# One block of zeros one place sooner, and the first load in two halves: a recurrence with a mixture of experts behind it

## The chip, the cores and the metric

The kernel runs on one core of a Trainium2 chip. The metric is the device time of one execution in microseconds (us); 213.54 us is the median of three runs before the change (213.47 to 214.17).

## The reference

What is computed is a gated recurrence over four sequences of 5056 tokens with 256 features, followed by a mixture of eight experts on its 20224 rows. Each expert keeps the 80 rows with the largest gate; all other rows of the output are zero.

```python
sig = 1.0 / (1.0 + np.exp(-f_logit))
f = lower_bound + (1.0 - lower_bound) * sig
for t in range(S):                      # h, y: (4, 256) at each t
    h = f[:, t] * h + (1.0 - f[:, t]) * x[:, t]
    y[:, t] = h
x = y.reshape(20224, 256)
logits = x @ w_gate                     # 8 experts
expert_idx = argmax(logits); gate_w = softmax(logits)[expert_idx]
out = zeros
for e in range(8):
    tok = the 80 tokens of expert e with the largest gate_w
    out[tok] = gate_w[tok] * (relu(x[tok] @ w1[e]) @ w2[e])
```

## The kernel before, in words

The first stage runs over 40 units of 512 tokens of one sequence. For each, "load" (line 233) issues two DMAs of 512 KB on SyncE's queue, f_logit into a tile f_t and x into a tile x_t, each of 128 partitions with 4 KB; eight ring slots hold them, so four units are loaded ahead. ScalarE takes the sigmoid (L242), GpSimd multiplies (L246), TensorE turns both (L252, L260), ScalarE forms the decay (L269) and VectorE scans (L277). Two small loads (w_gate and lower_bound, L215 and L217) stand behind the loads of unit 1; TensorE's first work, small_t (L223), turns them.

The output is some 20.7 MB and nearly all zero. One block of 512 KB is written from on-chip zeros by "clear"; "copied" (L132) copies it over the rest of the output, DRAM to DRAM, a block per call, and the calls are spread over the whole kernel as DMAs on SyncE's queue. The very last block is 256 KB.

The second stage ranks the rows (lines 496 to 703). The third, "experts" (L717), runs over the eight experts. The weights come as 32 halves of 512 KB, numbered k = 0 to 31 in the order in which they are loaded: w1 of expert 0, then, for each e, w1 of expert e+1 and w2 of expert e. Half k goes into ring slot 1 + k mod 7, so it waits for the reader of half k-7. Hence k = 26 and 27 are w1 of expert 7, 28 and 29 are w2 of expert 6, and 30 and 31 are w2 of expert 7 (31 is issued as two DMAs of 256 KB). "more" (L791) issues the next two halves, and behind half k as many blocks of zeros as BETWEEN (L530) names k; this list is the order written out by hand. "hidden" multiplies by w1 (L755), "relu" follows on ScalarE (L762) and VectorE (L763), "result" multiplies by w2 (L770), "finish" scales on VectorE (L778). At the end GpSimd issues eight "scatter"s (L783), indirect DMAs that write the 80 rows of each expert into the output; the code demands that all zeros are written by then. Scatters of experts 5 and 6 stand besides behind a matmul of result(7).

Work of one engine runs in the order in which the program issues it, and so do DMAs of SyncE's queue.

Of the kernel before, what the change touches and what calls it, by code (L numbers as in the profile page):

```python
# [17 lines left out]
P = 128  # L18
# [8 lines left out]
def kernel(  # L27
# [11 lines left out]
    nc = tc.nc  # L39
# [17 lines left out]
    def first(g):  # L57
        return g * G
# [27 lines left out]
    def slot(i, name):  # L86
        return ring[i].tile([P, R * D], F32, name=name, tag="buf")
# [44 lines left out]
    def copied():  # L132

        at = written[0]
        n = min(P * ZH, TOTAL - at)
        if n:
            z = 2 * ZH if n % (2 * ZH) == 0 else D
            nc.sync.dma_start(out=out_flat[ds(at, n)].rearrange("(p k) -> p k", k=z),
                              in_=out_flat[:n].rearrange("(p k) -> p k", k=z))
            written[0] += n  # L140
# [14 lines left out]
    def tiles(ap, b, g):  # L155
        return ap[b, ds(min(first(g), S - G), G)].rearrange("(p r) d -> p r d", r=R)
# [6 lines left out]
    with tc.tile_pool(name="gsm", bufs=1) as gsm:  # L163
# [3 lines left out]
        xs, fs, sts, uts, sps, ups, lgs, lss, lts, eqs = ({} for _ in range(10))  # L167
# [65 lines left out]
        def load(n):  # L233
            g, b = divmod(n, B)
            fs[n] = slot(2 * n % NSLOT, "f_t").rearrange("p (r d) -> p r d", r=R)
            nc.sync.dma_start(out=fs[n], in_=tiles(f_logit, b, g))
            xs[n] = slot((2 * n + 1) % NSLOT, "x_t").rearrange("p (r d) -> p r d", r=R)
            nc.sync.dma_start(out=xs[n], in_=tiles(x, b, g))

# [163 lines left out]
        with tc.tile_pool(name="plg", bufs=1, space=PSUM) as plg, \  # L403
             tc.tile_pool(name="plt", bufs=1, space=PSUM) as plt:
            with tc.tile_pool(name="pss", bufs=2, space=PSUM) as pss, \
                 tc.tile_pool(name="psu", bufs=3, space=PSUM) as psu:
                for n in range(-AHEAD, n_unit):
                    unit(load, n + AHEAD)
                    m = n + AHEAD
                    if m == 1:  # L410
# [34 lines left out]
                    if n > 0 and n % B == 0:  # L445
                        g = n // B - 1
# [7 lines left out]
            with tc.tile_pool(name="pct", bufs=4, space=PSUM) as pct:  # L454
                cts = {}

                def turn(*runs):
                    ct = pct.tile([P, 4 * P], F32, name="ct", tag="ct")
                    for g0, g1 in runs:
                        turned(ct[:, ds((g0 - runs[0][0]) * P, (g1 - g0) * P)], g0, g1)  # L460
                        cts[g0] = ct, runs[0][0]
                    return ct
# [18 lines left out]
                b = turn((4, 6))  # L481
# [44 lines left out]

    w_sb = {}
    RANKING = 12
    BETWEEN = (7, 8, 8, 14, 15, 20, 21, 25, 28)
    for k, key in enumerate(halves_of[:NSLOT - 1]):  # L530
        w_sb[key] = half(*key)
        copied()
# [184 lines left out]
    def experts(again):  # L717
        with tc.tile_pool(name="mp", bufs=2) as mp, \
# [72 lines left out]
            def more(m):  # L791
                for _ in range(2 * m):
                    if late:
# [3 lines left out]
                        if not again:  # L797
                            for _ in range(BETWEEN.count(k)):
                                copied()
# [44 lines left out]
    with tc.If(unsure > 0):  # L844
        with tc.tile_pool(name="all", bufs=1) as sel, \
# [31 lines left out]
            for e in range(E):  # L877
                nc.gpsimd.indirect_dma_start(
                    out=tok[:, ds(e, 1)], out_offset=None, in_=id_list,
# [54 lines left out]
```

## Time and profile before

| What | us |
|---|---|
| median of three runs | 213.54 |
| the profiled execution, its own time | 212.61 |
| its span, first to last instruction | 210.8 |
| TensorE busy | 178.6 (85%) |
| VectorE busy | 156.0 (74%) |
| GpSimd busy | 143.2 (68%) |
| ScalarE busy | 133.4 (63%) |

The profile is of one execution. PE is TensorE's matmuls, PEld its weight loads, DVE is VectorE, ACT is ScalarE, POOL is GpSimd and SP is SyncE; a "q" behind a name is that engine's queue, which hands work out. A tile name with an arrow, as w_sb<-in_moe_w_dram, is what an instruction writes and reads. In brackets behind an instruction stands the idle time of its engine and what ended it. All times count from the start of the span. The queue of hardware DMAs moved 79.45 MB, which is 94.1% of what 16 DMA engines' time allows over the span.

### The profile page before, as it was taken

Reading aid. Unit: us, or ns where it says so; the run is one execution under the profiler, and the core shown is the slowest. Engines: PE = TensorE matmul, PEld = TensorE weight load, DVE = VectorE, ACT = ScalarE, POOL = GpSimd, SP = SyncE. Lnnn points to the kernel's source line nnn. Section 1 sums busy time; section 2 is a strip of 40 time slices with the busy share of each in tenths; the row PEclk is TensorE's granted clock in tenths of the full one; section 3 lists DMA queues with packets and bytes.
Section 4 is the critical chain, followed back from the end, with each engine's and each line's share of the span. In section 5 each row is a group of like instructions: output and inputs, shape, how many; then the busy total and the mean of one; then the engine's idle time right before and its main releaser. Section 6 shows DMA issues by size and latency. Waiting matters only on the chain.

```text
span 210.8 us, 6578 instructions
## 1 busy us (share of the span) xinstructions
PE 178.6 (85%) x2091; PEld 140.2 (66%) x2091; DVE 156.0 (74%) x399; ACT 133.4 (63%) x420; POOL 143.2 (68%) x287
## 2 busy tenths in 40 slices
PE   0499989997999999989999886689999697989870
PEld 0498868785878778777878763355586475767540
DVE  5159969999998999899798999975678756461010
ACT  4279789797787778777979872615666555360000
POOL 4848779799797889769897982416666565620372
PEclk9999999999999999999999999797999999999998
DMA  5999999999999999999999999999999999999621
GB/s 214 419 364 398 411 419 448 386 444 394 410 409 414 384 423 375 399 450 386 433 375 408 428 393 371 419 414 432 424 403 404 424 404 420 413 408 410 237 74 51
DMA packets 21362, 80.60 MB, mean 382 GB/s; under 512 B 2580, under 2 KB 2710, under 8 KB 20888
## 3 DMA queue, kind: packets, MB, share of 16 engines
q1 hardware_dynamic: 20936, 79.45, 94.1%
q0 software_dynamic: 384, 0.66, 1.1%
q8 instruction: 18, 0.29, 0.5%
q14 instruction: 24, 0.20, 0.2%
HBM read 72.62 MB, written 21.36 MB: 446 GB/s over the span
## 4 chain that ended last, share of the span: by engine, by line
DMA 34%; PE 33%; ACT 11%; DVE 8%; issue 5%; POOL 4%; ACTq 1%; POOLq 0%; SPq 0%; DVEq 0%
DMA w_sb<-in_moe_w_dram 19%; PE sp L252 11%; PE up L260 9%; DMA x_t<-in_x_dram 8%; PE lg L290 6%; DMA f_t<-in_f_logit_dram 6%; ACT h_all L269 5%; PE lt L314 2%; ACT xe L735 2%; POOL x_t L246 2%; DVE h_all L277 2%; ACT ls L299 2%; PE y_ps L770 2%; POOL out_dram L783 2%; PE h_ps L755 1%
## 5 line engine op out<-in xcount | busy, mean ns | idle before, releaser
L246 POOL TENSOR_TENSOR x_t<-f_t,x_t 128x1024 f32<-128x1024 f32 x40 | 94.8, 2373 | 21.1 <-DMA x_t<-in_x_dram 12.5
L277 DVE TENSOR_TENSOR_SCAN h_all<-h_all,up 128x512 f32<-128x512 f32 (+1 forms) x80 | 95.8, 1245 | 10.4 <-PE up L260 6.5
L269 ACT ACTIVATE h_all<-sp,nomlb 128x512 f32<-128x512 f32 (+1 forms) x80 | 50.3, 678 | 13.6 <-PE sp L252 12.8
L242 ACT ACTIVATE f_t<-f_t 128x1024 f32<-128x1024 f32 x40 | 42.4, 1059 | 11.6 <-DMA f_t<-in_f_logit_dram 9.8
L260 PE MATMUL up<-ident,x_t 128*128 128x128 f32 x320 | 43.8, 279 | 3.1 <-DVE h_all L277 1.8
L252 PE MATMUL sp<-ident,f_t 128*128 128x128 f32 x320 | 45.4, 287 | 0.0
L252 PEld LDWEIGHTS sp<-ident,f_t 128*128 128x128 f32 x320 | 35.9, 145 | 7.7 <-issue 7.3
L260 PEld LDWEIGHTS up<-ident,x_t 128*128 128x128 f32 x320 | 37.0, 144 | 5.0 <-DVE h_all L277 2.9
L735 ACT COPY xe<-h_all 128x2 f32 x256 | 25.4, 191 | 14.6 <-issue 14.1
L735 POOL COPY xe<-h_all 128x2 f32 x192 | 24.4, 187 | 14.6 <-issue 8.3
L770 PE MATMUL y_ps<-w_sb,hid 128*80 128x256 f32 x128 | 29.5, 382 | 4.6 <-DMA w_sb<-in_moe_w_dram 4.6
L735 DVE COPY xe<-h_all 128x2 f32 x192 | 22.6, 176 | 12.2 <-issue 11.0
L770 PEld LDWEIGHTS y_ps<-w_sb,hid 128*80 128x80 f32 x128 | 18.4, 150 | 13.5 <-issue 3.4
L290 PE MATMUL lg<-h_all,wg 128*32 128x128 f32 (+1 forms) x640 | 26.5, 282 | 0.8 <-ACT ls L299 0.6
L755 PEld LDWEIGHTS h_ps<-xe,w_sb 128*64 128x64 f32 x512 | 18.3, 138 | 5.7 <-issue 3.0
L755 PE MATMUL h_ps<-xe,w_sb 128*64 128x80 f32 x512 | 19.5, 234 | 1.0 <-DMA w_sb<-in_moe_w_dram 0.6
L290 PEld LDWEIGHTS lg<-h_all,wg 128*32 128x32 f32 x640 | 15.4, 108 | 7.2 <-issue 4.9
L783 POOL DMA_INDIRECT out_dram<-y,goal x8 | 7.5, 939 | 11.1 <-DMA w_sb<-in_moe_w_dram 9.0
L161 PE MATMUL warm<-h_all,ident 128*128 128x512 f32 x18 | 11.9, 807 | 0.0
L778 DVE TENSOR_SCALAR y<-y_ps,gates 80x256 f32<-80x256 f32 x8 | 3.8, 477 | 10.9 <-PE y_ps L770 10.5
L762 ACT ACTIVATE hid<-h_ps 128x320 f32<-128x320 f32 x8 | 3.5, 435 | 11.3 <-PE h_ps L755 5.8
L314 PE MATMUL lt<-ident,ls 128*128 128x128 f32 (+1 forms) x40 | 7.3, 306 | 3.7 <-ACT ls L299 3.7
(128 smaller groups left out, 98.8 us busy)
## 6 DMA issues: line engine op xcount, KB each, us to landing
f_t<-in_f_logit_dram SPq DMA_DIRECT2D x40, 512.0 KB, 6.4
x_t<-in_x_dram SPq DMA_DIRECT2D x40, 512.0 KB, 6.9
w_sb<-in_moe_w_dram SPq DMA_DIRECT2D x31, 512.0 KB, 9.9
out_dram<-out_dram SPq DMA_DIRECT2D x26, 512.0 KB, 9.8
out_dram<-zbuf SPq DMA_DIRECT2D x12, 512.0 KB, 10.4
out_dram<-h_all SPq DMA_DIRECT2D x1, 512.0 KB, 8.2
w_sb<-in_moe_w_dram SPq DMA_DIRECT2D x2, 256.0 KB, 8.8
out_dram<-out_dram SPq DMA_DIRECT2D x1, 256.0 KB, 9.4
```

What stands on the lines that cost most here:

```text
L161: nc.tensor.matmul(warm, ident, h_all[:, 0, :4 * P], start=True, stop=True)
L242: nc.scalar.activation(s_t, s_t, ACT.Sigmoid, scale=-1.0)
L246: nc.gpsimd.tensor_tensor(u_t, sts[n], u_t, ALU.mult)
L252: nc.tensor.transpose(ps[:, ds(r * P, P)], sts[n][:, r, ds(o * P, P)], ident)
L260: nc.tensor.transpose(ps[:, r::R], uts[n][:, r, ds(o * P, P)], ident)
L269: nc.scalar.activation(columns(n, o).rearrange("p (k r) -> p k r", r=R), sps.pop((n, o)).rearrange("p (r k) -> p k r", r=R)[:, P - run(n / ...
L277: nc.vector.tensor_tensor_scan(h, h, ups.pop((n, o)), h_all[:, o, ds(spot(n - B) + G - 1, 1)] if n >= B else 0.0, ALU.mult, ALU.add)
L290: nc.tensor.matmul(lgs[g][ds(q * LC, LC), b, :k].rearrange("p (m i) -> p m i", i=2), wg[:, o], pairs[:, :, q], start=o == 0, stop=o == DC ...
L735: copy(X[e][:, :, ds(k + j, 1)], h_all[:, :, ds(v, 1)])
L755: nc.tensor.matmul(ps[i][ds(s * H, H), c], wo[o][:, at:at + J * (H - 1) + 1:J], xt[:, o], start=o == 0 and c == 0, stop=o == DC - 1, skip_ ...
L770: marks[e, c] = nc.tensor.matmul(y, hid[:, c], halves[c // CH][:, c % CH], start=c == 0, stop=c == FC - 1, skip_group_check=True)
L783: sent.append(nc.gpsimd.indirect_dma_start(out=out, out_offset=bass.IndirectOffsetOnAxis(ap=goal[:, ds(e, 1)], axis=0), in_=rows.pop(e), i ...
```

## The change

Two places differ. In BETWEEN the last number goes from 28 to 27, so the last block of zeros is issued behind half 27 and ahead of half 28. In "load", f_logit of unit 0 is loaded with two DMAs, of partitions 0 to 63 and of 64 to 127; all other loads are as they were.

```diff
-            nc.sync.dma_start(out=fs[n], in_=tiles(f_logit, b, g))
+
+            for p in range(0, P, P // 2 if n == 0 else P):
+                part = ds(p, P // 2 if n == 0 else P)
+                nc.sync.dma_start(out=fs[n][part], in_=tiles(f_logit, b, g)[part])
...
-    BETWEEN = (7, 8, 8, 14, 15, 20, 21, 25, 28)
+    BETWEEN = (7, 8, 8, 14, 15, 20, 21, 25, 27)
```

## Rows read from the trace of the kernel before

**Rows 1.** The page: span, DMA share in 40 slices, the scatters' DMA queue.

```profile
span 210.8 us, 6578 instructions
...
DMA  5999999999999999999999999999999999999621
...
q0 software_dynamic: 384, 0.66, 1.1%
```

**Rows 2.** The chain of waits from 186 us: start, us, what.

```profile
177.06 10.18 DMA w_sb<-in_moe_w_dram
...
188.74 9.88 DMA w_sb<-in_moe_w_dram
```

**Rows 3.** Timeline of GpSimd from 188.5: start, us, instruction, idle before it.

```profile
197.72 1.13 POOL L783 DMA_INDIRECT out_dram<-y,goal  x1 [8.96 <-DMA w_sb<-in_moe_w_dram]
199.15 0.92 POOL L783 DMA_INDIRECT out_dram<-y,goal  x1 [0.30 <-issue]
...
206.45 0.91 POOL L783 DMA_INDIRECT out_dram<-y,goal  x1 [0.30 <-issue]
```

**Rows 4.** Tile out_dram, DMAs issued from 187 to 188: issue to landing.

```profile
DMA to landing us min/median/max: 9.4/9.4/9.4
```

**Rows 5.** Line 783, instructions from 196 to 197.6: GpSimd's queue.

```profile
L783 POOLq EVENT_SEMAPHORE  x2: 42/42/43, 196.7 to 196.8; - x2
```

**Rows 6.** Timeline of SyncE's queue from 183 to 212.

```profile
183.46 1.95 SPq L517 DMA_DIRECT2D w_sb<-in_moe_w_dram  x2
186.80 0.38 SPq L523 DMA_DIRECT2D w_sb<-in_moe_w_dram  x1
187.26 0.52 SPq L138 DMA_DIRECT2D out_dram<-out_dram  x1
188.74 3.86 SPq L523 DMA_DIRECT2D w_sb<-in_moe_w_dram  x4
```

**Rows 7.** Tile w_sb, the DMA issued at 183.46 (k=26): issue to landing.

```profile
DMA to landing us min/median/max: 10.0/10.0/10.0
```

**Rows 8.** Timeline of all engines from 193: ScalarE, TensorE, VectorE.

```profile
195.58 0.44 ACT L762 ACTIVATE hid<-h_ps 128x320 f32<-128x320 f32 x1 [5.77 <-PE h_ps L755]
...
196.06 1.93 PE L770 MATMUL y_ps<-w_sb,hid 128*80 128x256 f32 x8
...
198.75 5.38 PE L770 MATMUL y_ps<-w_sb,hid 128*80 128x256 f32 x24 [0.76 <-DMA w_sb<-in_moe_w_dram]
...
204.17 0.48 DVE L778 TENSOR_SCALAR y<-y_ps,gates 80x256 f32<-80x256 f32 x1 [2.97 <-PE y_ps L770]
```

**Rows 9.** Line 842, behind the scatters in the program: GpSimd's queue.

```profile
L842 POOLq TENSOR_LOAD <-doubt x1: 294/294/294, 204.7 to 204.7; - x1
```

**Rows 10.** Timeline of SyncE's queue at the start.

```profile
0.73 0.39 SPq L236 DMA_DIRECT2D f_t<-in_f_logit_dram  x1
1.18 0.42 SPq L238 DMA_DIRECT2D x_t<-in_x_dram  x1
...
4.52 0.33 SPq L236 DMA_DIRECT2D f_t<-in_f_logit_dram  x1
...
11.33 0.33 SPq L236 DMA_DIRECT2D f_t<-in_f_logit_dram  x1
```

**Rows 11.** DMA issues from 0.5 to 1: KB, us to landing.

```profile
f_t<-in_f_logit_dram SPq DMA_DIRECT2D x1, 512.0 KB, 3.8
```

**Rows 12.** Windows: us, busy (count) by engine, then PEclk, DMA share, GB/s.

```profile
0.00:1.77 1.77, 0.00 (x0) 0.00 (x0) 0.85 (x8) 1.04 (x1) 1.06 (x9) 1.00 0.00 0
1.77:2.77 1.00, 0.00 (x0) 0.00 (x0) 0.96 (x5) 0.45 (x2) 1.00 (x3) 1.00 0.45 176
2.77:3.30 0.53, 0.00 (x0) 0.00 (x0) 0.46 (x3) 0.00 (x0) 0.45 (x6) 1.00 0.93 348
...
12.40:60.00 47.60, 45.31 (x526) 38.11 (x525) 43.54 (x39) 39.05 (x54) 39.55 (x18) 1.00 1.03 415
```

**Rows 13.** Timeline of TensorE at the start.

```profile
8.25 1.11 PE L223 MATMUL small_t<-ident,h_all 2*128 2x2 f32 x9 [8.25 <-POOL x_t L246]
```

## The prediction

> **What bounds the kernel now.** I read the page first: its second part shows the 16 DMA engines at nine tenths or more from the second slice to the 37th, while no compute engine is [rows 1]. The windows say the same with numbers: from 12.40 us on the DMA share is 1.03 at 415 GB/s [rows 12]. So the kernel is one long DMA stream with a head, in which it fills, and a tail, in which it has run out. Both edits touch an end, so I read the two ends and not the middle.
>
> The tail, from the chain of waits: the first half of w2 of expert 6 is the half k=28, the second k=29, those of expert 7 are 30 and 31; "result" multiplies a half only when it has landed. k=29 is issued at 188.74 and takes 9.88 us, landing at 198.62 [rows 2]. TensorE starts on it at 198.75 and works 5.38 us without a break through result(6) and result(7); VectorE's last y ends at 204.17 + 0.48 = 204.65 [rows 8]. But that is not what ends last. GpSimd issues the eight scatters: the first begins at 197.72, the second at 199.15, then every 1.21 us (0.91 busy, 0.30 between them) to the eighth at 206.45, with no wait between them [rows 3]. The eighth is handed over as soon as y(7) is there (GpSimd's queue is already at line 842 at 204.7 [rows 9]) and then lies 1.75 us behind its fellows. So the end of the span hangs on when the first scatter starts.
>
> What starts it? All scatters stand behind all zeros. The last block of zeros (256 KB) is issued at 187.26 [rows 6] and lands 9.4 us later [rows 4], at 196.66. GpSimd's queue passes its last two semaphore waits at 196.7 and 196.8 [rows 5], and the scatter runs 0.9 us after that. The timeline puts the wait down to a w_sb transfer; the one known to land next, k=29, comes 0.9 us after the start, so I read the last zeros as the true releaser.
>
> **Part one: the zeros, one half sooner.** No instruction is added. The block's DMA moves from behind k=28 to behind k=27 on SyncE's queue. Now SyncE ends the issue of k=27 at 183.46 + 1.95 = 185.41, waits, issues k=28 at 186.80 and the zeros at 187.26 [rows 6]. 187.26 is also when the eighth DMA before it lands: k=22, 177.06 + 10.18 = 187.24 [rows 2]; at the start the ninth DMA likewise goes at 4.52, when the first lands (0.73 + 3.8) [rows 10, 11]. So eight DMAs are out at most. After the change the zeros go at about 185.45, and k=28 inherits the wait for k=22: 187.26 instead of 186.80, 0.46 us later. Queued behind it on SyncE is k=29, which waits until 188.74 in any case. None of these issue times counts, since about 9.5 us of queue lie between issue and landing; what counts is the order in the queue.
>
> In the queue the zeros now pass one half. From k=26 (183.46 + 10.0 = 193.46 [rows 6, 7]) to the zeros (196.66) 3.20 us serve k=27, k=28 and the zeros, 2.5 halves of 512 KB: 1.28 us a half and 0.64 us for the zeros. New landing of the zeros: 196.66 - 1.28 = 195.38. First scatter: 197.72 - 1.28 = 196.44. Eighth: 206.45 - 1.28 = 205.17. Its data: y(7) is taken over at 204.7, and a scatter starts 0.30 us later, 205.0 at the soonest. So 0.17 us stay free, and the most that the scatters can gain is 206.45 - 205.0 = 1.45.
>
> What is late next is k=28. It lands where the zeros did, at 196.66, about 0.7 later than now. TensorE begins result(6) at 196.06 when ScalarE's relu (195.58 + 0.44) is done [rows 8]; now it would begin at 196.66 + 0.13 = 196.79, end at 198.72, and k=29 starts at 198.75 as before. So the cover is the wait for k=29, with 0.03 us to spare; beyond that, and beyond the 0.17 us above, each further 0.1 us costs 0.1. The earlier scatters also write while the last halves still come: all 384 packets of their queue take 1.1% of 16 engines' 210.8 us, 2.3 us, 0.29 us a scatter [rows 1]. One more of them before k=29 lands costs between 0 and 0.12 (0.29 less the free 0.17). I take 0, since only the lagging engines still work then. Part one: -1.28, with ends -1.45 and -0.79 (below).
>
> **Part two: the first load in two halves.** It adds one DMA issue on SyncE. f_t of unit 0 (0.73), x_t (1.18) and the others are issued 0.45 us apart [rows 10], so x_t, the next units and the small loads are issued up to 0.45 us later. Against that the trace shows a hole: from 1.77 to 2.77 the DMA share is only 0.45 at 176 GB/s, then 0.93 [rows 12]. Half of the engines begin a microsecond late. If two transfers of half the rows filled all of them at once, the stream would win up to 0.55 x 1.00 = 0.55 us. The sigmoid and x*f of unit 0 gain nothing that counts: TensorE's first work, small_t at 8.25 [rows 13], needs by the code only the identity and the small loads, which stand behind four loads (the trace names x*f of unit 0, which ends at the same time), and SyncE's next load waits until 11.33 [rows 10] for a slot. As the queue is full from 12.40 on, a shift of the stream goes through to the end whole. Ends: -0.55 and +0.45. No row shows a 64-partition load. The nearest say this: data first moves at 1.77, 1.04 us after the issue; x_t, issued at 1.63, could move from 2.67, and f_t at the full rate keeps the engines until 1.77 + 1.28 = 3.05, so the extra issue has 0.38 us of cover; and the half that is late now is late within one issue, which need not change. So I take 0.
>
> [...]
>
> **The sum.** 1.28 + 0 = 1.28 us. On the profiled execution (212.61 us, span 210.8) that is 211.33; on the median, which lies 0.93 above it, 213.54 - 1.28 = 212.26, call it 212.3.
>
> **Rivals.** (a) The cover breaks: k=29 landed 1.96 us behind the zeros [rows 2, 4], 0.68 more than a half takes. If that pause belongs to what follows the zeros and not to its moment, it falls on k=28: landing 197.34, result(6)'s first part 197.47 to 199.40, the rest 0.65 later, y(7) at 205.30, the eighth scatter at 205.66: gain 0.79, 212.75. For it: it came just there. Against: the halves before, as the 1.28 shows, had none. (b) The split costs its issue, 0.45, since x_t comes late to a stream that has just begun: gain 0.83, 212.7. For: the hole is at that very place. Against: the 0.38 us of cover. (c) The split closes the hole: 1.28 + 0.55, 211.7. (d) The scatters wait for a weight half, as the trace's label says, k=28 then landing later: part one gives nothing, 213.5. (e) Slower: a transfer of 64 partitions runs on half of the engines. Those then carry all of unit 0's f_t, one more 256 KB at 176 GB/s, 1.49 us, and x_t comes 0.45 us late: +1.94 - 1.28 = +0.66, 214.2. It decides once the split costs more than the 1.28 that the zeros give. For: in the first microsecond exactly half of the engines work. Against: all 16 run at full share soon after, with the same kind of load.
>
> **How the numbers follow.** Forecast 0.47; (a) 0.14, (b) 0.13, (c) 0.12, (d) 0.08, (e) 0.06. The range goes from 211.6 to 213.2; it leaves out (d) and (e). Within 0.3% (0.64 us, about what can be told here from no change) lie (d), half of (e), and about a third of (a) and (b), whose 0.8 is close to the bound: 0.20. Slower: 0.04. Faster: 0.76.
>
> **What would show it.** After the change the last zeros are issued near 185.4, before k=28, and land near 195.4; the first scatter starts near 196.4 and the eighth near 205.2, still 1.21 apart; result(7)'s y still ends near 204.65; k=28 lands near 196.7. The DMA share from 1.77 to 2.77 tells the split's part: 0.45 again means nothing gained. Wrong would be: an eighth scatter that waits for y(7), a k=29 that lands later, a first TensorE instruction after 8.4, or a first scatter still at 197.7.

## The result, and the profile after

The kernel became slower, not faster.

| What | before | after |
|---|---|---|
| median, us | 212.82 (20 runs, 211.75 to 214.17) | 214.51 (20 runs, 212.54 to 216.68) |
| ratio | 1 | 1.0068 [1.0041, 1.0094] |
| a second comparison (e8) | 1 | 1.0098 [1.0055, 1.0140] |
| span of the execution shown | 210.8 | 212.6 |
| first work of TensorE | 8.25 [rows 13] | 9.41 |
| first scatter | 197.72 [rows 3] | 197.80 |
| y(7) done | 204.65 [rows 8] | 206.76 |
| eighth scatter | 206.45 [rows 3] | 207.04 |

The forecast was 212.3 with a range of 211.6 to 213.2, so the time lies above the range. The ratio leaves out, as slow runs, four runs of the changed kernel that lie over 1.5% above its fastest, and since the execution profiled at first was one of them, the rows of the changed kernel are those of a second profile of the same program (e8, 214.44 us).

The head, windows as in [rows 12]: us, busy (count) of PE, PEld, DVE, ACT, POOL, then PEclk, DMA share, GB/s. First the windows of before that go with them:

```profile
3.77:4.77 1.00, 0.00 (x0) 0.00 (x0) 0.36 (x3) 0.25 (x1) 0.00 (x0) 1.00 1.02 418
...
1.77:6.77 5.00, 0.00 (x0) 0.00 (x0) 2.22 (x11) 1.50 (x3) 2.37 (x8) 1.00 0.88 349
...
40.00:50.00 10.00, 9.24 (x120) 7.48 (x121) 9.59 (x11) 8.00 (x10) 7.93 (x5) 1.00 1.02 417
```

Then the changed kernel, from the moment at which data first moves:

```profile
1.77:2.77 1.00, 0.00 (x0) 0.00 (x0) 0.96 (x5) 0.45 (x2) 1.00 (x3) 1.00 0.63 111
...
3.77:4.77 1.00, 0.00 (x0) 0.00 (x0) 0.36 (x3) 0.00 (x0) 0.00 (x0) 1.00 0.88 172
...
1.77:6.77 5.00, 0.00 (x0) 0.00 (x0) 2.22 (x11) 1.50 (x3) 1.46 (x7) 1.00 0.90 273
```

The last two columns are the ones to read together. The share counts the time of the packets that start in the window, so it can pass 1; the rate counts their bytes. From 3.77 to 4.77 the share is 0.88 and the rate 172 GB/s, where before has 1.02 and 418. By these numbers 4 KB take 16 x 0.88 x 4096 B / 172 GB/s = 0.34 us of an engine, against 0.16 in before. Over the five microseconds the share is 0.90 against 0.88 and the rate 273 against 349. So a share of busy engines does not tell how much they move. (The 94.1% beside the 79.45 MB, ahead of the prediction, is such a share of time too, and not a share of the bytes that could have been moved.)

The changed kernel's issue queue of SyncE at the start, against [rows 10], and TensorE's first work, against [rows 13]:

```profile
0.73 1.22 SPq L239 DMA_DIRECT2D f_t<-in_f_logit_dram  x2
1.99 0.58 SPq L241 DMA_DIRECT2D x_t<-in_x_dram  x1
```

```profile
9.41 1.12 PE L223 MATMUL small_t<-ident,h_all 2*128 2x2 f32 x9 [9.41 <-DMA h_all<-in_moe_w_gate_dram]
```

The two halves take 1.22 us to issue, where one load took 0.39, and x_t follows at 1.99, 0.81 later than before. TensorE begins 1.16 later, and what releases it is the small load that stands behind the first loads.

The tail of the changed kernel: SyncE's queue, the scatters, and y(7), against [rows 6, 3, 8].

```profile
184.94 1.70 SPq L520 DMA_DIRECT2D w_sb<-in_moe_w_dram  x2
187.35 0.52 SPq L138 DMA_DIRECT2D out_dram<-out_dram  x1
188.61 5.42 SPq L526 DMA_DIRECT2D w_sb<-in_moe_w_dram  x5
```

```profile
197.80 1.13 POOL L786 DMA_INDIRECT out_dram<-y,goal  x1 [7.82 <-DMA w_sb<-in_moe_w_dram]
...
207.04 0.92 POOL L786 DMA_INDIRECT out_dram<-y,goal  x1 [0.78 <-issue]
```

```profile
206.28 0.48 DVE L781 TENSOR_SCALAR y<-y_ps,gates 80x256 f32<-80x256 f32 x1 [3.98 <-PE y_ps L773]
```

The zeros now go behind half 27 and ahead of half 28, as written. The eighth scatter, which in before came 1.80 us after y(7) was done, comes 0.28 after it: the scatters no longer lie behind. But y(7) itself is done 2.11 later, and the span ends 5.84 after it (212.6 - 206.76), where it ended 6.15 after it before (210.8 - 204.65). Where the 2.11 arise is told by y(6), the row ahead of y(7) on VectorE, in before and in the changed kernel:

```profile
200.72 0.48 DVE L778 TENSOR_SCALAR y<-y_ps,gates 80x256 f32<-80x256 f32 x1 [4.08 <-PE y_ps L770]
```

```profile
201.82 0.48 DVE L781 TENSOR_SCALAR y<-y_ps,gates 80x256 f32<-80x256 f32 x1 [3.77 <-issue]
```

y(6) is 1.10 later, much like TensorE's first work; from y(6) to y(7) it then takes 4.46 us (206.28 - 201.82), where before took 3.45 (204.17 - 200.72). So three things are to be explained: a microsecond lost ahead of y(6), another between y(6) and y(7), and a gain of more than a microsecond in the scatters that the end hardly shows.

### The profile page after: what moved, and what is told of

The parts are those of the page before. It is cut to its first block, busy times and chain, and to the rows that moved or that the text cites. A ratio compares the mean times of both kernels' runs of the same rounds, so it can differ in the third digit from the quotient of the medians.

```text
span 214.5 us, 6582 instructions
## 1 busy us (share of the span) xinstructions
PE 180.1 (84%) x2091; PEld 141.1 (66%) x2091; DVE 155.3 (72%) x399; ACT 133.4 (62%) x420; POOL 143.5 (67%) x287
## 3 DMA queue, kind: packets, MB, share of 16 engines
q1 hardware_dynamic: 20952, 79.45, 93.3%
## 4 chain that ended last, share of the span: by engine, by line
PE 42%; DMA 31%; ACT 10%; DVE 8%; issue 3%; POOL 2%; SPq 1%; DVEq 0%; POOLq 0%; ACTq 0%
DMA w_sb<-in_moe_w_dram 14%; PE sp L255 10%; DMA f_t<-in_f_logit_dram 9%; PE up L263 8%; PE y_ps L773 6%; PE lg L293 6%; ACT h_all L272 5%; PE h_ps L758 4%; DMA x_t<-in_x_dram 4%; PE warm L161 3%; DMA h_all<-in_moe_w_gate_dram 3%; PE lt L317 2%; ACT f_t L245 2%; ACT ls L302 2%; PE slots L690 2%
## 5 line engine op out<-in xcount | busy, mean ns | idle before, releaser
L263 PEld LDWEIGHTS up<-ident,x_t 128*128 128x128 f32 x320 | 36.5, 143 | 6.3 <-POOL x_t L249 3.8
```

The lines of the kernel that those rows point to most:

```text
L263: nc.tensor.transpose(ps[:, r::R], uts[n][:, r, ds(o * P, P)], ident)
```

## The experiments

All ratios are to the kernel before, run on the same chip beside the experiment, with 95% intervals. The two parts of the change come first, each alone.

**e1, the zeros alone.**

```diff
-    BETWEEN = (7, 8, 8, 14, 15, 20, 21, 25, 28)
+    BETWEEN = (7, 8, 8, 14, 15, 20, 21, 25, 27)
```

> The kernel before with the zeros' half alone: the last block of zeros behind half 27, no split. If the loss is the split's (all theories that blame the head): the last zeros land 1.28 us sooner, the first scatter starts near 196.4 and the eighth near 205.2, ratio 0.994 (1.0 to 1.3 us faster). If the zeros' move itself is at fault (half 28 late, rival a or worse): no faster than before, ratio 1.000 to 1.003, and result(7)'s y ends later than 204.65.

Measured: 1.0012 [0.9985, 1.0039], median 213.06 against 213.29; the profiled execution (212.53 us) has a span of 210.7. Its rows: SyncE, the scatters, y(6) and y(7).

```profile
182.44 1.96 SPq L517 DMA_DIRECT2D w_sb<-in_moe_w_dram  x2
185.02 0.52 SPq L138 DMA_DIRECT2D out_dram<-out_dram  x1
```

```profile
195.54 1.13 POOL L783 DMA_INDIRECT out_dram<-y,goal  x1 [7.79 <-DMA w_sb<-in_moe_w_dram]
...
204.80 0.91 POOL L783 DMA_INDIRECT out_dram<-y,goal  x1 [0.83 <-issue]
```

```profile
199.67 0.48 DVE L778 TENSOR_SCALAR y<-y_ps,gates 80x256 f32<-80x256 f32 x1 [4.04 <-issue]
204.04 0.48 DVE L778 TENSOR_SCALAR y<-y_ps,gates 80x256 f32<-80x256 f32 x1 [3.90 <-PE y_ps L770]
```

Against before the first scatter starts 2.18 sooner, the eighth 1.65 sooner and 0.28 after y(7) is done (204.04 + 0.48 = 204.52), the same 0.28 as in the changed kernel. Not all of this is the zeros': in this execution half 26 is issued 1.02 sooner too (182.44 against 183.46), and for the first scatter 2.18 - 1.02 = 1.16 is left. y(6) comes 1.05 sooner, as half 26 does, so half 28 being late cost nothing up to there. y(7) comes only 0.13 sooner: 4.37 us lie between y(6) and y(7), as 4.46 did in e8. TensorE's matmuls are shown to end at 203.09, 0.95 ahead of y(7), and what held y(7) is not shown. That the moved zeros do it is not shown either: e6 below has them and takes 3.46 (203.35 - 199.89), and e3, without them, takes 3.97 (206.11 - 202.14). The span of e1 is 210.7 against 210.8. The scatters were not what ended last, or not alone.

**e2, the split alone.** The first part of the change's diff, with BETWEEN as before.

> The kernel before with the split of the first load alone. If the loss is the split's: slower by the change's loss plus what the zeros gave, 1.4 + 1.3 = 2.7 us, ratio 1.012 to 1.013, TensorE's first work near 9.5 instead of 8.25 and every landing some 1 to 2 us later to the end. If the split costs its issue alone: 0.45 us, ratio 1.002.

Measured: 1.0100 [1.0066, 1.0135], median 214.96, 2.1 us [1.4, 2.9] by the ratio. Two windows of its head and TensorE's first work:

```profile
3.77:4.77 1.00, 0.00 (x0) 0.00 (x0) 0.35 (x3) 0.00 (x0) 0.00 (x0) 1.00 1.12 201
...
1.77:6.77 5.00, 0.00 (x0) 0.00 (x0) 2.21 (x10) 1.50 (x3) 1.45 (x7) 1.00 0.94 265
```

```profile
9.65 1.12 PE L223 MATMUL small_t<-ident,h_all 2*128 2x2 f32 x9 [9.65 <-DMA h_all<-in_moe_w_gate_dram]
```

So the loss is all the split's, and the two parts add up within their intervals: 0.12% and 1.00% alone, 0.68% and 0.98% in the two comparisons of both. From 3.77 to 4.77 the share is 1.12 at 201 GB/s, half of the 418 of before: 0.37 us of an engine for 4 KB, against 0.16. In the five windows 5 x (349 - 265) = 420 KB are missing, about 1.0 us of stream at the 415 GB/s of [rows 12].

**e3 and e4, the same load in two transfers, but otherwise cut:** by columns (128 partitions, half of the columns each), and by even and odd partitions (64 partitions each, spread over all).

```diff
-            nc.sync.dma_start(out=fs[n], in_=tiles(f_logit, b, g))
+            for r in range(0, R, R // 2 if n == 0 else R):
+                some = ds(r, R // 2 if n == 0 else R)
+                nc.sync.dma_start(out=fs[n][:, some], in_=tiles(f_logit, b, g)[:, some])
```

```diff
-            nc.sync.dma_start(out=fs[n], in_=tiles(f_logit, b, g))
+            for p in range(2 if n == 0 else 1):
+                part = slice(p, P, 2 if n == 0 else 1)
+                nc.sync.dma_start(out=fs[n][part], in_=tiles(f_logit, b, g)[part])
```

> The first load as two transfers of all 128 partitions and half of the columns (2 KB a partition each), zeros as before: the same two issues and bytes as the split by partitions. If the cost is the extra issue and what it pushes back on SyncE's queue: as slow as the split by partitions (ratio 1.010 or more). If the cost is that all 16 engines write into one half of the partitions: the packets keep their usual time per byte, the DMA share after 1.77 us is as before or better, and at most 0.45 us is lost, ratio 0.999 to 1.002.

> The first load as two transfers of 64 partitions, the even ones and then the odd ones, zeros as before. Same number of issues, partitions and rows a transfer as in the change, but each transfer is spread over the whole of the partitions. If the place in memory (one half of the partitions) is what slows the packets: packets at their usual 0.16 us and a loss of at most 0.45 us, ratio up to 1.002. If it is the number of 64 partitions or the issue: as slow as the change's split, ratio 1.010 or more.

Measured: 1.0070 [1.0037, 1.0103] by columns, 1.0119 [1.0076, 1.0163] by even and odd. All three cuts of the very first load cost, 0.70% by columns, 1.19% by even and odd and 1.00% by halves (e2), and the intervals of the last two overlap. So at this place the half of the partitions can't be the whole cause; the extra issue, or what it does to the loads behind it, has a part. By columns the two issues take 0.86 us and x_t goes at 1.64; by even and odd they take 1.22 and x_t goes at 2.00, as in the change. What the cuts themselves do is told by the same three at a place where the issue can't matter.

**e7, e10 and e13, the three cuts in the middle of the stream.** f_t of the 16 units 8 to 23 is split in each, all else is as before: e7 by halves of the partitions (the change's loop with `8 <= n < 24` for `n == 0`), e10 by columns (e3's loop with it), e13 by even and odd (e4's with it). There the stream is full (a share of 1.03 at 415 GB/s from 12.40 on [rows 12]), so an issue more should delay nothing, as e10 and e13 bear out (ratios of 1.0027 and 1.0022).

> The kernel before with f_t of units 8 to 23 loaded as two transfers of 64 partitions, 16 splits in the middle of the stream, where several loads are queued ahead; the first load whole. If a transfer into one half of the partitions moves at half the rate (201 GB/s against some 410, as in the change's first 2 us), each split costs up to 1.3 us of stream and the kernel is 5 to 20 us slower, less what engines that run apart from one another save. If the split costs only at the head, by issues that come late and find nothing queued: ratio 1.000 to 1.003.

> The kernel before with f_t of units 8 to 23 as two transfers of all 128 partitions and half of the columns: the same 16 extra issues as in the splits by partitions in the stream. [...]

> The kernel before with f_t of units 8 to 23 as two transfers of 64 partitions, even and odd ones: the same number of issues, partitions and rows as the splits by halves in the stream (ratio 1.107, 24 us). If the place of the partitions (one half of the memory) makes the loss: ratio 1.000 to 1.005, as with the splits by columns. If transfers of 64 partitions are slow in themselves: 1.08 to 1.11.

Measured: halves 1.1068 [1.0994, 1.1141], columns 1.0027 [0.9994, 1.0060], even and odd 1.0022 [0.9990, 1.0053]. A window of e7 and, behind it, of e13; the same window of before stands in the section on the result:

```profile
40.00:50.00 10.00, 7.07 (x66) 5.46 (x67) 5.64 (x6) 5.54 (x9) 4.80 (x3) 0.80 1.03 277
```

```profile
40.00:50.00 10.00, 9.45 (x123) 7.67 (x122) 9.05 (x12) 7.84 (x11) 7.87 (x5) 1.00 1.02 406
```

The DMA share is 1.03 and 1.02, but 277 GB/s against 406: 0.24 us of an engine for 4 KB, against 0.16. By the ratio, 16 splits cost 0.1068 x 212.4 = 22.7 us, 1.42 a split [1.32, 1.52]; at half the rate 512 KB would take 1.28 us more (the duration of a half from the prediction), so a half rate would be nearly all of it. Neither the number of transfers (e10) nor 64 partitions as such (e13) costs anything that can be told from nothing: what is left is that the partitions of one transfer are 0 to 63 or 64 to 127. (The cuts differ in DRAM too: a half of e7 reads one block of 256 KB, a part of e13 every second 4 KB. No run separates the two.) Why such a transfer moves at about half the rate (201 GB/s at a share of 1.12 in e2) is not shown.

**e11 and e12, what an issue and a late x_t cost at the head.** e11 puts one small load (lower_bound, 1 KB) ahead of the first f_t; e12 cuts the second load, x_t of unit 0, by columns and leaves f_t whole.

```diff
+                nc.sync.dma_start(out=small[:, E * P:],
+                                  in_=lower_bound.rearrange("(o p) -> o p", p=P))
...
-            nc.sync.dma_start(out=small[:, E * P:], in_=lower_bound.rearrange("(o p) -> o p", p=P))
```

```diff
-            nc.sync.dma_start(out=xs[n], in_=tiles(x, b, g))
+            for r in range(0, R, R // 2 if n == 0 else R):
+                some = ds(r, R // 2 if n == 0 else R)
+                nc.sync.dma_start(out=xs[n][:, some], in_=tiles(x, b, g)[:, some])
```

> The kernel before with the small load of lower_bound (1 KB) moved from behind unit 1 to the very front of SyncE's queue: the first load is whole and keeps its 512 KB, but comes one issue later. If one more issue at the front is the price by itself: data first moves 0.3 to 0.5 us later and the kernel is 0.3 to 0.5 us slower, ratio 1.001 to 1.003. If the head's loss comes with any change of the order there (starved engines): 1.007 or more.

> The kernel before with the second load, x_t of unit 0, as two transfers of all 128 partitions and half of the columns; the first load whole. If the split by columns of the first load lost 0.7% because the third issue found the engines empty (only 2 x 256 KB ahead of it), then here 512 KB more stand ahead and no hole opens: DMA share about 1 from 3 us on, ratio 0.999 to 1.002. If any extra issue among the first loads opens a hole: a DMA share below 0.9 somewhere between 3 and 6.8 us and ratio 1.005 to 1.008.

Measured: 1.0039 [1.0004, 1.0073] and 1.0040 [1.0002, 1.0077]. In e11 f_t goes 0.42 later:

```profile
1.15 0.37 SPq L235 DMA_DIRECT2D f_t<-in_f_logit_dram  x1
```

and the kernel is 0.83 us [0.09, 1.55] longer, an interval with room for the 0.42 and for twice that. So this issue at the head was not free, where the prediction took it at 0 with 0.45 as the bound. The cuts by halves (1.00% [0.66, 1.35]) and by even and odd cost more than that; the cut by columns (0.70% [0.37, 1.03]) can't be told from it.

The profile of e12 (214.61 us, above its median of 213.37) shows that the loss is not made at the head alone. Windows of before, of e2 and of e12:

```profile
40.00:60.00 20.00, 18.89 (x231) 15.62 (x232) 19.07 (x19) 16.08 (x22) 16.71 (x9) 1.00 1.04 420
```

```profile
40.00:60.00 20.00, 18.50 (x225) 15.00 (x225) 18.72 (x18) 16.13 (x23) 16.83 (x8) 1.00 0.99 394
```

```profile
40.00:60.00 20.00, 18.49 (x226) 14.98 (x225) 18.80 (x18) 16.08 (x22) 16.71 (x8) 1.00 0.99 374
```

From 1.77 to 12.40 e12 moves 360 GB/s against 365 in before, and from 12.40 to 40 it moves 415 against 412. From 40 to 60 it falls behind by 20 x (420 - 374) = 920 KB, about 2.2 us of stream, and e2 by 520 KB. e1, e5 and e6, whose head is that of before, move 415 to 418 there. Why a changed head should show so late, and in some executions more than in others, is not shown.

**e14 and e15, one execution more of e4 and of e3, with its profile,** for the reason of the cost at the head.

> The first load by even and odd partitions, once more for a second trace. If the first loads' queue runs empty regularly after a split first load: a DMA share under 0.9 somewhere between 3 and 6 us again, and unit 0's x_t landing after 6.2. If it was an accident of one execution: a share near 1 throughout.

> The first load by columns, once more for a second trace. If regular: a DMA share under 0.9 between 3 and 6 us again (it was 0.43 to 0.63) and x_t of unit 0 landing after 7 us. If an accident: a share near 1 throughout and x_t landing near 5.8.

Measured: 215.23 us by even and odd, 213.60 by columns. Windows of e14, by even and odd:

```profile
3.77:4.77 1.00, 0.00 (x0) 0.00 (x0) 0.36 (x3) 0.00 (x0) 0.00 (x0) 1.00 0.41 139
4.77:5.77 1.00, 0.00 (x0) 0.00 (x0) 0.00 (x0) 0.31 (x1) 0.00 (x0) 1.00 0.51 201
...
1.77:6.77 5.00, 0.00 (x0) 0.00 (x0) 2.22 (x10) 1.50 (x3) 1.45 (x7) 1.00 0.66 213
```

Here it is the share that is low (0.41 at 139 GB/s): the engines are idle, where in e2 they are busy at about half rate (1.12 at 201 GB/s). The DMA issued at 1.99 for x_t lands 6.8 us later, in before (issued at 1.18) 4.5 later:

```profile
x_t<-in_x_dram SPq DMA_DIRECT2D x1, 512.0 KB, 6.8
```

In e15 the same five microseconds carry 303 GB/s at 0.91, and from 3.77 to 4.77 its share is 0.99 at 258 GB/s, so there the engines are not idle. The earlier profiles of the same two kernels carry 304 (e4) and 243 (e3) in the five microseconds: how much is lost varies from execution to execution. The cut by even and odd, not to be told from free in the stream (0.22% for 16 in e13), left the engines at the head of e14 with a share of 0.66 over the five microseconds, where before has 0.88; why x_t's data come so much later than its issue stays open.

**e5 and e6, the end without the branch.** Behind the scatters the program reads a flag and, if it is set, runs a second pass (lines 842 to 900); it is not set here. In e5 these lines, the flag's load and the branch with them, are removed from the kernel before, in e6 from the kernel with the zeros behind half 27.

```diff
-    unsure = nc.values_load(doubt, min_val=0, max_val=4 * P,
...
-    with tc.If(unsure > 0):
...
```

> The kernel before without the second pass of the ranking (lines 842 to 900, run only when the ranking is uncertain, which it is not here) and so without the load of the flag and the branch over that code. Theory J (the end of the span hangs on GpSimd's branch, which its queue reaches only when it has handed over the scatter of y(7) and which then takes 3.2 us): the end comes with the scatters instead, whose eighth still starts near 206.4, so little is won, 0 to 0.6 us, ratio 0.997 to 1.000. Theory S (the end hangs on the eighth scatter, as predicted): no change either, 1.000.

> The same kernel without the second pass and its branch, with the last zeros behind half 27. Theory J: with the branch gone the zeros' gain shows at last: the eighth scatter starts at y(7)'s end, near 204.8, and the end comes 1.3 to 1.6 us sooner than in the same kernel with the zeros behind half 28; against the kernel before 0.990 to 0.994. If the zeros' move is worth nothing for another reason (late weight halves): the same time as the kernel without the branch and the zeros behind 28, within 0.3 us.

Measured: e5 0.9974 [0.9944, 1.0004], e6 0.9884 [0.9840, 0.9927], medians 211.95 and 210.43 beside 212.39. Line 844 of the kernel before, on the queues of GpSimd, VectorE and TensorE (ns min/median/max, first to last start in us):

```profile
L844 POOLq EVENT_SEMAPHORE  x6: 17/30/43, 208.3 to 208.8; - x6
...
L844 DVEq EVENT_SEMAPHORE  x2: 21/21/21, 207.8 to 207.9; - x2
...
L844 PEldq COMPARE_BRANCH  x1: 3872/3872/3872, 201.7 to 201.7; - x1
L844 DVEq COMPARE_BRANCH  x1: 76/76/76, 204.7 to 204.7; - x1
L844 POOLq COMPARE_BRANCH  x1: 53/53/53, 205.0 to 205.0; - x1
```

The same line of e1 on GpSimd, whose scatters came 1.65 sooner:

```profile
L844 POOLq EVENT_SEMAPHORE  x6: 17/30/43, 208.2 to 208.7; - x6
...
L844 POOLq COMPARE_BRANCH  x1: 53/53/53, 204.9 to 204.9; - x1
```

and of the changed kernel (line 847 there):

```profile
L847 POOLq EVENT_SEMAPHORE  x6: 17/30/43, 210.2 to 210.6; - x6
...
L847 POOLq COMPARE_BRANCH  x1: 53/53/53, 207.2 to 207.2; - x1
```

This is the second path to the end. GpSimd hands over the last scatter when y(7) is there, loads the flag (204.7 [rows 9]), takes the branch at 205.0 in 53 ns, and its next instruction begins at 208.3. VectorE stands between 204.7 and 207.8; TensorE's branch is shown with 3.87, from 201.7, while its matmuls still run. About 2.5 us of end work follow (208.3 to 210.8). The branch starts with y(7) and not with the scatters, and so e1, with y(7) 0.13 sooner, resumes only 0.1 sooner: no packet of its scatters starts after 207.4, and its end still comes at 210.7. In that gap the trace shows packets of instructions (before, DMA queues from 205.1 to 208.2: packets, MB, share):

```profile
q0 software_dynamic: 118, 0.23, 25.7%
q8 instruction: 1, 0.02, 2.0%
q14 instruction: 2, 0.02, 1.7%
```

and none where there is no branch (e5, from 202.7 to 209.0):

```profile
q0 software_dynamic: 192, 0.33, 17.2%
```

That GpSimd waits for these packets is not shown: the trace gives the 3.2 us and the three packets, but nothing that ends the wait.

Without the branch the end follows the eighth scatter by 3.95 us in both:

```profile
205.15 0.91 POOL L783 DMA_INDIRECT out_dram<-y,goal  x1 [0.30 <-issue]
```

```profile
204.75 0.91 POOL L783 DMA_INDIRECT out_dram<-y,goal  x1 [0.31 <-issue]
```

(e5, span 209.1, and e6, span 208.7.) With that step the scatters of before alone would have ended the span at 206.45 + 3.95 = 210.40, and those of e1 at 204.80 + 3.95 = 208.75. The branch ended it at 210.8 and 210.7. These two sums are estimates, since the 3.95 is from kernels without the branch. By them the branch was the later path in before, by 0.4 us, with which e5's 0.26% is compatible, and in e1 it was later by 1.95 us. Without the branch moving the zeros is worth 1.5 us by the medians of e5 and e6, 0.90% (1.9 us) by their ratios, and 1.3 us [0.5, 2.0] by the means of their runs: the gain that the prediction worked out at 1.28 is there, and the branch hides it. The two executions shown differ by 0.4 alone, because the one of e5 is the fastest of its twelve (210.84) and has half 26 out at 182.28, 0.63 ahead of e6 (182.91); hence its eighth scatter at 205.15, where 206.4 was expected. Counted from half 26, the eighth scatter of e6 comes 1.03 sooner (22.87 against 21.84).

**e9, the branch ahead of the scatters.** The zeros stand behind half 27, and the scatters are moved behind the second pass (5 and 6 then stand behind no matmul), so that its branch would be over while the zeros are still on their way.

```diff
-            for e in range(E):
-                scatter(e, apart.get(e))
...
+    for e in range(E):
+        sent.append(nc.gpsimd.indirect_dma_start(
```

> Nothing left out: the last zeros behind half 27, no split, and the eight scatters moved behind the second pass, once for both ways, so that GpSimd takes its branch while it waits for the zeros and not after the last scatter (the second pass then only makes new rows and row numbers; scatters 5 and 6 no longer stand behind a matmul). Theory J: the 3.2 us branch is hidden, the end comes with the scatters: 1.5 to 2.5 us sooner than the kernel before, ratio 0.988 to 0.993. If the end of the second pass makes GpSimd wait for the other engines, the scatters start only after y(7), near 205, and the kernel is slower, ratio 1.01 to 1.02.

Measured: 1.0427 [1.0380, 1.0475], 221.84 us. Its first scatter, and line 831, which is its branch:

```profile
207.85 1.13 POOL L881 DMA_INDIRECT out_dram<-y,goal  x1 [19.27 <-DVEq L831]
```

```profile
L831 POOLq EVENT_SEMAPHORE  x6: 17/30/43, 193.5 to 198.4; - x6
L831 DVEq EVENT_SEMAPHORE  x2: 21/21/21, 207.5 to 207.6; - x2
...
L831 DVEq COMPARE_BRANCH  x1: 76/76/76, 204.4 to 204.4; - x1
L831 POOLq COMPARE_BRANCH  x1: 45/45/45, 188.5 to 188.5; - x1
```

GpSimd's own branch is hidden as meant (188.5, resumed at 193.5), but at the end of the branched part GpSimd waits 19.27 us for VectorE, which makes y(7) first and comes out of its branch at 207.5. The scatters then begin 10 us later than before. This version does not save the gain.

**e8, the changed kernel again,** for a second profile and a second comparison; no edit.

> The changed kernel once more, for a second trace of it. Ratio 1.004 to 1.010. If the head's loss is regular: data first moves near 2.1 us, x_t of unit 0 lands 1 to 2 us later than before, TensorE's first work is near 9.6, and the first scatter, the branch and the end are late by about the same.

Measured: 1.0098 [1.0055, 1.0140], 214.46 us. Its rows are those of the section on the result.

## Why the prediction was wrong, point by point

**Where the forecast starts.** Its base, the median of three runs (213.54), lies 0.72 above the median of twenty (212.82). So the miss is larger than 214.51 - 212.3 = 2.2 tells: 1.28 was forecast as a gain, and 1.4 [0.9, 2.0] by the ratio was lost.

**What bounds the kernel.** Right in the main: a full DMA stream with a head and a tail. That a shift of the head goes through to the end fits e8, with its first work 1.16 late and y(6) 1.10 late. It is not the whole, since e12 and e2 lose part of their time from 40 to 60 us, and e8 loses another 1.0 between y(6) and y(7); neither is explained.

**Part one, up to the scatters: right.** The zeros were issued at 185.02 (e1) against 185.4 forecast, the first scatter started at 195.54 against 196.4, the eighth at 204.80 against 205.2, and half 28 being late cost nothing up to y(6). Counted from half 26, which e1 issues 1.02 sooner than before, the first scatter gained 1.16 of the 1.28; the eighth came as soon as y(7) let it. Rival (a) falls, since result(6) was not held up, though y(7) then came 0.92 later behind y(6) than in before; rival (d) falls, since the scatters did move. Two of the signs of being wrong were seen: the eighth scatter waited for y(7) in e1 and e8, and TensorE began after 8.4 in e8 (9.41), but also in e1 (8.42) and e6 (8.51), whose head is that of before.

**Part one, from the scatters to the end: wrong, and the step can be named.** The prediction says that "the end of the span hangs on when the first scatter starts". It had no row for what ends last; the eighth scatter is the last row of the timeline, a view that leaves branches and semaphores out. The row that speaks against it was in hand: GpSimd's load of the flag at 204.7 [rows 9], read only as proof that the eighth scatter had been handed over. Following that queue one line on shows a branch at 205.0 and the next instruction at 208.3. With the branch path already the later one (210.8 against 210.4), scatters that come sooner gain nothing: -1.28 becomes +0.3 [-0.3, 0.8] (e1: +0.12% [-0.15, 0.39]).

**Part two, the split: wrong.** Taken at 0 with a bound of +0.45; it costs 2.1 us [1.4, 2.9]. Three terms were wrong. The extra issue is no 0.45: the pair took 1.22 us and x_t went 0.81 later; rival (b), the issue alone at 0.45, falls short as well. The "0.38 us of cover" was not there: x_t's data came late, and the engines meanwhile worked at about half rate (e2: 201 GB/s at a share of 1.12; e8: 172 at 0.88) or stood idle (e14: 139 at 0.41). And the half rate itself, which rival (e) named, was priced at 6 in 100. That its price for the split, 1.94, is close to what was measured is in part luck. Its mechanism, half of the engines at work, is shown by no run; from 3.77 to 4.77 the share is 0.88 (e8) and 1.12 (e2) instead while 4 KB take about twice as long (0.34 and 0.37 us of an engine against 0.16), and the half rate accounts for about 1.0, where it has 1.49. Its 214.2 is near the measured 214.51 because two errors partly cancel, the 1.28 that it grants the zeros and the base that is 0.72 too high. The argument against it, that "all 16 run at full share soon after, with the same kind of load", does not bear on it: later loads span 128 partitions, and a share does not tell the rate (1.03 stood beside 277 GB/s in e7 and beside 415 in before). How the 2.1 splits into half rate (420 KB, about 1.0 us), lateness at the head and the loss from 40 to 60 us is not settled, for e3 and e4, which aren't cut into halves of the partitions, lose 1.5 and 2.5 us. The step that failed is the 0 for the split; why a cut of the first load costs this much stays in part open.

**The hole at the head** of 0.45 [rows 12] tells nothing of what the head moves. e1, whose head is the same, has

```profile
1.77:2.77 1.00, 0.00 (x0) 0.00 (x0) 0.97 (x4) 0.45 (x2) 1.00 (x3) 1.00 0.94 98
...
1.77:6.77 5.00, 0.00 (x0) 0.00 (x0) 2.21 (x10) 1.50 (x3) 2.49 (x8) 1.00 1.00 351
```

and by 6.77 both have moved the same (349 and 351 GB/s). In the eight executions with this head (before, e1, e5, e6, e7, e9, e10, e13) the share from 1.77 to 2.77 lies between 0.45 and 1.01 and the rate between 90 and 176 GB/s, and none moves more than the 176 of before; over the five microseconds all move 348 to 356. So "half of the engines begin a microsecond late" is not borne out, nor what rival (e) has for it, that "in the first microsecond exactly half of the engines work". Rival (c) rested on it and falls: there was nothing to close.

**The sum with the measured terms:** +0.3 [-0.3, 0.8] for the zeros, with the branch still there, and +2.1 [1.4, 2.9] for the split give +2.4 where the two comparisons of the whole change show +1.4 [0.9, 2.0] and +2.1 [1.2, 3.0].

## What to carry to other kernels

Before a tail is shortened, follow each queue to its last instruction, branches and end work included: here the path through a branch ended some 0.4 us (an estimate) behind the one that was shortened and hid all of a gain of 1.3 to 1.9. Before a transfer is cut, each cut is tried alone: in the full stream a cut into partitions 0 to 63 and 64 to 127 cost 1.42 us here, and cuts by columns or by even and odd partitions cost nothing that could be told, while at the first load the three cost 0.7 to 1.2%. A DMA share near 1 is read with the GB/s beside it: 1.03 stood beside 277 in e7 and beside 415 in before.

## What the runs showed of the hardware

- In the full stream a transfer of 512 KB in two halves of the partitions cost 1.42 us [1.32, 1.52], at a DMA share of 1.03 (e7); 16 cuts by columns cost 0.27% (e10) and 16 by even and odd partitions 0.22% (e13), neither to be told from nothing. From 40 to 50 us an engine's time for 4 KB was 0.24 us in e7, against 0.16 in before.
- In before GpSimd's queue shows its next instruction 3.2 us after the branch over the second pass (lines 842 to 900; from 205.0 + 0.05 to 208.3; 2.9 in e8) and VectorE's 3.0 after it, although the branch itself is shown with 53 and 76 ns; TensorE's is shown with 3.9, part of it while its matmuls still run.
- At the head the issue of one half of 256 KB took about 0.61 us and that of the x_t behind it 0.58 (e8), where whole loads took 0.39 and 0.42 [rows 10]; two halves by columns took 0.43 each, and the x_t behind them 0.43 (e3).
- The first microsecond of the stream differed between executions with the same head (a share of 0.45 to 1.01 from 1.77 to 2.77, in eight), with nearly the same bytes moved by 6.77 (348 to 356 GB/s).
